# One half step of the attention behind every half group of the first two expert units

## Chip, cores and metric

The kernel runs on one core of a Trainium2 chip. The metric is the device time of one execution in microseconds, the median of the runs. The page of the profile names the engines as PE (TensorE), DVE (VectorE), ACT (ScalarE), POOL (GpSimd) and SP (SyncE, which issues most DMAs). "L500" is line 500 of the kernel before.

## What is computed

Three layers run one behind another on 1152 tokens (2 batches of 576).

```python
# attention, 8 heads of 64, on q, k, v [2, 8, 576, 64]
q_d, k_d, v_d = means over 4 neighbouring positions          # 144 positions
out_up = repeat(softmax(q_d @ k_d.T / 8) @ v_d, 4)           # the coarse part
out_local = softmax(mask(|i - j| < 4, q @ k.T / 8)) @ v      # the local part
x = (out_up + out_local) as [1152, 512]
# experts: P [1152, 8] from exp(x @ w_gate), 8 rounds of row and column normalization
out = sum over e of P[:, e] * (relu(x @ w1[e]) @ w2[e])      # w1[e] 512 x 1024, w2[e] 1024 x 512
# gated layer
result = ((out @ w_a) * (out @ w_b)) @ w_out                 # inner width 1536
```

## The kernel before

All large products keep float32 accuracy in three passes: both factors are split into a high and a low part (`xh`, `xl` for the tokens, `hi`, `lo` for the weights, `gh`, `gl` for the hidden layer) and hi·hi, lo·hi and hi·lo are summed in PSUM. An expert is cut into two units of 512 hidden columns; there are 16 units and then 6 units of the gated layer.

**The stage of the change** is the part in which attention and the first two expert units share the engines. Tokens come in three blocks of 384 (`NB`, `TB`). For a block and a unit there are four groups (`g_plain`, `f` = 0 to 3): 12 matmuls of 384 columns (4 contraction tiles by 3 passes, `g_part`) into one PSUM bank, then the relu on ScalarE (L500, writes `gh`) and the low part on VectorE (L501, writes `gl`). Then come three output tiles for each unit (`o_moe`, `o_mm`): 12 matmuls of 512 columns each, and one VectorE instruction adds the result to `acc` (L541, L543). Groups and tiles use two PSUM banks in turn.

**Attention** is a software pipeline in the generator `side()`. `order` lists 24 steps (a batch, a third of its positions, a pair of heads); eight of them bring new keys (third 0): indices 0, 2, 4, 6, 10, 12, 14 and 15. Iteration `s` has two half steps, each ended by a `yield`:

- first half: loads for step s+2 on SP (`load_q`, `load_k`, `load_v`); `a1(s)` transposes the queries on TensorE (L990), and where the step brings keys also six key tiles (L1004); `c3(s-3)` and `a2(s)` are copies out of PSUM on ScalarE (L1148; keys L1011, L1012; queries L1023); `b4(s-2)` is four VectorE instructions (L1111, L1112, L1115, L1119) and one on GpSimd (L1116); `d3` is one on ScalarE (L1185) and one on GpSimd (L1186); `b2(s-1)` is two maxima on VectorE (L1089, L1092); `a3(s)` sums keys (L1048, where there are new ones) and queries (L1037) over four positions on VectorE.
- second half, for s from 11 (`TURN`) on: `a4(s)` scales the summed keys on ScalarE (L1059); TensorE then runs `b1(s)` (a mask matmul, then local scores; needs the queries of `a2`), `d1(s-3)` (values), `b1c(s)` (coarse scores, tile `kd`; needs the sums of `a3` and `a4`) and `c1(s-2)` (transposes of the softmax, L1129, L1134); `d2a` and `b3` run on ScalarE (L1169, the exponentials L1099 and L1102), `d2` and `c2` on VectorE (L1175, L1140).

When a block of tokens is complete, `logits` follows in two halves: eight matmuls and a copy on ScalarE (L1203), then three transposes (L1208) and a copy. Attention's own PSUM tiles rotate through six banks (`psa`). Each engine takes its instructions in the order in which this Python program writes them down.

**What sets the order.** After every group and every output tile the loop calls `step()` (L1472). It adds `SIDE` = 1.5 to `turn` and, if two are due, runs two half steps one directly behind the other, with one piece of weight preparation (`run_first`: a cast on ScalarE, L138, and a subtraction on VectorE, L139) written between them; in the steady pattern that is none, two, two, two. A pair that starts inside the pipeline is the second half of one step and the first half of the next. `load_some`, called once for each half step, hands one weight DMA to SP. Up to the first block (23 half steps) attention runs without this loop, with two groups of block 0 filled in by `g_early`; at the start of block 1 two groups are opened (9 of 12 matmuls) ahead of the loop (`begun`). Before the third block the attention is closed and the gating of the experts takes the place of the half steps (`mid`).

Of the kernel before, what the change touches and what calls it, by code (L numbers as in the profile page):

```python
# [8 lines left out]
F32 = mybir.dt.float32  # L9
# [11 lines left out]
def attn_moe_glu_kernel(  # L21
# [16 lines left out]
    nc = tc.nc  # L38
# [6 lines left out]
    KT = DM // 128  # L45
# [34 lines left out]
    ident = const.tile([128, 128], F32, name="ident")  # L80
# [249 lines left out]
    for i, w in enumerate((w_a, w_b, w_out)):  # L330
        t = dram.tile(list(w.shape), F32, name=f"w32_{i}")
# [86 lines left out]
    units = []  # L418
    for e in range(E):
        for hf in range(2):  # L420
            u = Unit()
# [8 lines left out]
    for g in range(GU):  # L430
        u = Unit()
# [21 lines left out]
    def g_part(u, ps, b, f, kts):  # L453

        cols = slice(b * TB, (b + 1) * TB)
        for kt in kts:
            w = u.w[f // 2, kt // 2]
            o = (kt % 2) * 256 + (f % 2) * 128
            a_h, a_l = w.hi[:, o:o + 128], w.lo[:, o:o + 128]
            parts = (a_h, xh), (a_l, xh), (a_h, xl)  # L460
            for k, (l, r) in enumerate(parts):
                mm(ps, l, r[:, kt, cols], kt == 0 and k == 0, kt == KT - 1 and k == 2)
        M.pe += 0.52 * len(kts)

    def g_open(u, b, f):
        ps = bank("g")[:, :TB]
        g_part(u, ps, b, f, range(KT - 1))
        return ps

    def g_early(u, b, banks):  # L470
# [14 lines left out]
                if kt < KT - 1:  # L485
                    yield

    def g_plain(u, n, b, f, mid, ps=None, full=False):

        gh, gl = GP[0][n], GP[1][n]  # L490
        if ps is None:
            ps = g_open(u, b, f)
        if not full:
            g_part(u, ps, b, f, (KT - 1,))
        for j in range(2):
            u.w[f // 2, j].use()
        if closed:
            pump(0.0)
        mid()
        nc.scalar.activation(out=gh[:, f], in_=ps, func=AF.Relu)  # L500
        nc.vector.scalar_tensor_tensor(  # L501
            out=gl[:, f], in0=ps, scalar=0.0, in1=gh[:, f].bitcast(F32),
            op0=ALU.max, op1=ALU.subtract,
        )
        act(0.5)
        dve(0.56)

    def o_mm(u, gh, gl, t):
        ps = bank("o")
        k = 0  # L510
        for f in (0, 2, 3, 1) if u.no == 4 else (0, 1):
            sl = slice(t * 128, (t + 1) * 128)
            a_h, a_l = gh[f][:, sl], gl[f][:, sl]
            w = u.o[f]
            for l, r in ((a_h, w.hi), (a_h, w.lo), (a_l, w.hi)):
                mm(ps, l, r, k == 0, k == 3 * u.no - 1)
                k += 1
        M.pe += 0.683 * u.no
        for w in u.o:
            w.use()  # L520
        return ps

    def o_moe(u, gh, gl, t, tt, mid=None, first=False):
        if u.e > 0:
            while gens[0] is not None:
                side_step()
        ps = o_mm(u, gh, gl, t)
        if mid:
            if closed:
                pump(0.0)  # L530
            mid()
        if not first:
            pump()
        a = acc[tt]
        if u.e == 0:
            if u.hf == 0 and closed:
                nc.scalar.copy(out=a, in_=ps)
                act(0.65)
                return
            if u.hf == 0:  # L540
                nc.vector.tensor_copy(out=a, in_=ps)  # L541
            else:
                nc.vector.tensor_tensor(out=a, in0=ps, in1=a, op=ALU.add)  # L543
        else:
            if u.e == 1 and u.hf == 0:
                nc.scalar.mul(out=a, in_=a, mul=P[:, tt, 0:1])
                act(0.65)
            nc.vector.scalar_tensor_tensor(  # L548
                out=a, in0=ps, scalar=P[:, tt, u.e:u.e + 1], in1=a, op0=ALU.mult, op1=ALU.add
            )  # L550
        dve(0.76)
        if first:
            pump()
# [328 lines left out]
    at = attn_stack.enter_context(tc.tile_pool(name="at", bufs=3, side="right"))  # L882
# [101 lines left out]

    def a1(i, b, u, hp):

        pq = psa.tile([128, 512], F32, tag="at", name="at")
        qn = q_nat.pop((b, u, hp))
        for j in range(2):
            nc.tensor.transpose(  # L990
                pq[:, j * 96:(j + 1) * 96], qn[:, j].rearrange("p h d -> p (h d)"), ident[:96, :96]
            )
        pk = pk2 = None
        if not i:
            warm(1)
        if u == 0:
            kn = k_nat[b, hp]
            pk = pq[:, 192:480]
            if not i:
                pk = psa.tile([128, 512], F32, tag="at", name="at")[:, 0:288]  # L1000
            pk2 = psa.tile([128, 512], F32, tag="at", name="at")
            for j in range(6):
                o = (pk if j < 3 else pk2)[:, j % 3 * 96:j % 3 * 96 + 96]
                nc.tensor.transpose(o, kn[:, j].rearrange("p h d -> p (h d)"), ident[:96, :96])  # L1004
        pA[i] = pq, pk, pk2

    def a2(i, b, u, hp):
        pq, pk, pk2 = pA.pop(i)
# [252 lines left out]
    def side():  # L1261
        n = len(order)
        done_l = 0

        def do(st, j):
            if 0 <= j < n:
                st(j, *order[j])

        for s in range(n + 5):
            if s == 5:  # L1270
                wg32 = load_gate()
            if s == 9:
                gate_weights(wg32)
            if s + 2 < n:
                load_q(s + 2)
                if order[s + 2][1] == 0:
                    load_k(order[s + 2][0], order[s + 2][2])
            if s in FETCH_VD:
                load_vd(0, FETCH_VD.index(s))
            if s in LOAD_V:  # L1280
                load_v(LOAD_V[s])
            last = s >= 4 and (s - 3) % (2 * HP) == 0
            do(a1, s)
            if s <= TURN:
                do(b1, s - 1)
                do(b1c, s - 1)
            if last:
                do(d3, s - 4)
            do(c3, s - 3)
            do(a2, s)  # L1290
            do(b4, s - 2)
            if not last:
                do(d3, s - 4)
            do(b2, s - 1)
            do(a3, s)
            yield
            do(a4, s)
            if s >= TURN:
                do(b1, s)
            do(d1, s - 3)  # L1300
            if s >= TURN:
                do(b1c, s)
            do(d2a, s - 3)
            do(b3, s - 1)
            do(c1, s - 2)
            do(d2, s - 3)
            do(c2, s - 2)
            if s in SUM_VD:
                sum_vd(0, SUM_VD.index(s))
            if 0 <= s - 2 < n and order[s - 2][:2] == (1, 0):  # L1310
                sum_vd(1, order[s - 2][2])
            if 0 <= s - 1 < n and order[s - 1][:2] == (1, 0):
                load_vd(1, order[s - 1][2])
            yield
            while done_l <= ready[0]:
                yield from logits(done_l)
                done_l += 1
                yield

    TURN = 11  # L1320
    FRONT = 10
    V_PAIRS = (0, 2, 4, 6, 16, 18, 20, 22)
    PAIRS = V_PAIRS[2:]
# [30 lines left out]
    with tc.manual_schedule():  # L1354
# [58 lines left out]
        def run_first(n):  # L1413
            while n and wq:
                if len(units[1].o) == 4 and (wq[0].slot or not wq[0].ok()):
                    return
                n -= run(wq).slot
# [52 lines left out]
        share = [0, 0, 1, 1, 1, 1, 2, 2, 1, 2, 1]  # L1470

        def step():  # L1472
            nonlocal turn
            if not closed:
                turn += SIDE
                n = 0
                while n < 2 and (turn >= 2 or n):
                    turn -= 1
                    side_step()
                    n += 1  # L1480
                    if n == 1:
                        run_first(share.pop(0) if share else 1)
                if not n:
                    run_first(share.pop(0) if share else 1)
            else:
                pump()

        def mid():
            if closed:
# [4 lines left out]
        for b in range(NB):  # L1494
# [23 lines left out]
            for n in range(2):  # L1518
                while len(units[n].w) < 2:
                    run_first(1)  # L1520
                full = bool(begun)
                if n == 0 and not closed and not full:
                    begun = {f: g_open(units[n], b, f) for f in range(2)}
                for f in range(4):
                    while len(units[n].w) < 4 and f > 1:
                        run_first(1)
                    g_plain(units[n], n, b, f, mid, begun.get(f), full and f < 2)
                    step()
                begun = {}
            per = TB // 128  # L1530
            firsts = [[
                lambda n=n, t=t, b=b: o_moe(
                    units[n], *([G[n][:, f] for f in range(4)] for G in GP), t, b * per + t, mid)
                for t in range(per)
            ] for n in range(2)]
            for n in range(2 if b < NB - 1 else 1):
# [145 lines left out]
```

## Time and profile before

| | |
|---|---|
| median of 3 runs | 1052.09 us (1051.04 to 1054.85) |
| the profiled execution: its time | 1052.0 us |
| its span, first to last instruction | 1050.2 us |
| granted TensorE clock, mean | 1.000 |
| TensorE busy (matmuls) | 1040.3 us |
| VectorE, ScalarE, GpSimd busy | 657.7, 481.3, 527.2 us |

The span is what the profile shows; 1.8 us lie around it. A row of a timeline gives the start, the duration, the engine, the line, the tiles written and read, the shape and the count; what stands in brackets is the engine's idle time before it and what ended it. A matmul's duration is longer than the distance to the next one, because matmuls overlap: distances between starts tell what the stream costs.

### The profile page before, as it was taken

To read this page: it belongs to the slowest core of one execution; us is meant where nothing else is said; L and a number is where in the kernel's file an instruction comes from. 1 tells how busy PE (TensorE), PEld (TensorE's weight loads), DVE (VectorE), ACT (ScalarE), POOL (GpSimd) and SP (SyncE) were. 2 spreads that over 40 slices of the span, in tenths; PEclk is the share of its full clock that TensorE was granted. 3 is DMA by queue.
4 is the path that set the end of the run, shared out by engine and by line. 5 is a ranking of instruction groups with operands and counts; after the bars stand their busy time and mean duration, and the time that the engine had idled before them with its cause. 6 is when DMAs were issued, how large, how long until landed. Compare 5 with 4: busy or idle time off the path is not lost.

```text
span 1050.2 us, 18523 instructions
## 1 busy us (share of the span) xinstructions
PE 1040.3 (99%) x6940; PEld 938.0 (89%) x6940; DVE 657.7 (63%) x1333; ACT 481.3 (46%) x1168; POOL 527.2 (50%) x531
## 2 busy tenths in 40 slices
PE   8999999999999999999999999999999999999998
PEld 6887888989998998999899998999899899999997
DVE  7785638666566565656665565656544685767664
ACT  6764514664454444445444454545333744333320
POOL 5533236646474644647465554646444545655521
PEclk9999999999999999999999999999999999999999
DMA  9552001242423323242333323232210102221002
GB/s 191 147 150 73 16 1 41 71 129 67 128 83 112 102 89 105 66 127 84 109 91 103 105 66 106 85 117 83 71 61 21 41 21 61 61 61 41 31 11 90
DMA packets 80728, 84.53 MB, mean 80 GB/s; under 512 B 35328, under 2 KB 54784, under 8 KB 80640
## 3 DMA queue, kind: packets, MB, share of 16 engines
q1 hardware_dynamic: 79456, 83.07, 26.8%
q8 instruction: 54, 0.88, 0.3%
q10 hardware_dynamic: 1184, 0.30, 0.1%
q14 instruction: 34, 0.28, 0.1%
HBM read 71.54 MB, written 11.80 MB: 79 GB/s over the span
## 4 chain that ended last, share of the span: by engine, by line
PE 94%; DVE 3%; DMA 1%; ACT 1%; issue 1%; SPq 0%; POOL 0%; DVEq 0%; ACTq 0%
PE g L61 89%; PE at L61 3%; DMA kn<-in_k_dram 1%; PE at L1129 1%; PE at L1134 1%; DMA vw<-in_v_dram 0%; PE g L855 0%; DVE w L139 0%; DVE kd L1048 0%; DMA raw<-w 0%; ACT w L138 0%; DVE pdn L1119 0%; PE at L990 0%; ACT p L1099 0%; DVE rsum L1111 0%
## 5 line engine op out<-in xcount | busy, mean ns | idle before, releaser
L61 PE MATMUL g<-w,gh 128*128 128x512 f32 x1314 | 407.8, 391 | 0.0
L61 PE MATMUL g<-xh,w 128*128 128x256 f32 (+2 forms) x1472 | 315.9, 300 | 0.0
L692 POOL TENSOR_TENSOR gl<-G,gh 128x256 fp32r<-128x256 f32 (+1 forms) x216 | 178.1, 834 | 249.8 <-ACT gh L690 243.7
L61 PEld LDWEIGHTS g<-w,gh 128*128 128x128 f32 x1314 | 239.3, 188 | 44.0 <-DVE w L139 0.3
L61 PE MATMUL g<-w,gl 128*128 128x512 f32 x657 | 257.2, 392 | 0.0
L61 PEld LDWEIGHTS g<-xh,w 128*128 128x128 f32 x1472 | 242.6, 188 | 2.4
L61 PE MATMUL g<-xl,w 128*128 128x256 f32 (+2 forms) x736 | 219.7, 299 | 0.0
L696 DVE TENSOR_TENSOR G<-g,G 128x256 f32<-128x256 f32 (+1 forms) x400 | 168.3, 451 | 68.6 <-PE g L61 36.7
L61 PE MATMUL g<-Th,w 128*128 128x256 f32 (+1 forms) x960 | 207.4, 293 | 0.3 <-DVE G L696 0.2
L139 DVE TENSOR_TENSOR w<-raw,w 128x512 fp32r<-128x512 f32 x129 | 116.6, 914 | 79.8 <-ACT w L138 79.2
L61 PEld LDWEIGHTS g<-Th,w 128*128 128x128 f32 x960 | 159.6, 188 | 3.3 <-issue 0.9
L548 DVE SCALAR_TENSOR_TENSOR acc<-g,P,acc 128x512 f32<-128x512 f32 x126 | 94.2, 748 | 94.1 <-PE g L61 90.7
L61 PEld LDWEIGHTS g<-w,gl 128*128 128x128 f32 x657 | 123.3, 188 | 26.4
L61 PE MATMUL g<-Tl,w 128*128 128x256 f32 (+1 forms) x480 | 140.5, 293 | 0.0
L61 PEld LDWEIGHTS g<-xl,w 128*128 128x128 f32 x736 | 138.0, 188 | 2.6 <-issue 0.2
L690 ACT CAST gh<-G 128x256 fp32r<-128x256 f32 (+1 forms) x216 | 93.7, 434 | 100.7 <-DVE G L706 85.8
L138 ACT CAST w<-raw 128x512 fp32r<-128x512 f32 x181 | 109.7, 622 | 62.2 <-POOL raw L269 47.7
L688 ACT ACTIVATE G<-G 128x256 f32<-128x256 f32 (+1 forms) x168 | 74.2, 442 | 103.1 <-DVE G L696 103.1
L139 POOL TENSOR_TENSOR w<-raw,w 128x512 fp32r<-128x512 f32 x52 | 68.5, 1326 | 58.3 <-ACT w L138 58.3
L61 PEld LDWEIGHTS g<-Tl,w 128*128 128x128 f32 x480 | 90.2, 188 | 2.1
L381 POOL TENSOR_TENSOR dec<-dec 128x384 int32<-128x384 int32 x48 | 49.5, 1031 | 77.5 <-ACT dec L357 52.3
L139 POOL TENSOR_TENSOR w<-s,w 128x512 fp32r<-128x512 f32 x40 | 55.7, 1393 | 21.1 <-ACT w L138 21.0
(178 smaller groups left out, 992.4 us busy)
## 6 DMA issues: line engine op xcount, KB each, us to landing
raw<-in_moe_w_dram SPq DMA_DIRECT2D x128, 256.0 KB
w<-dec SPq DMA_DIRECT2D x48, 192.0 KB
dec<-in_moe_w_a_dram SPq DMA_DIRECT2D x16, 384.0 KB
dec<-in_moe_w_b_dram SPq DMA_DIRECT2D x16, 384.0 KB
dec<-in_moe_w_out_dram SPq DMA_DIRECT2D x16, 384.0 KB
raw<-w SPq DMA_DIRECT2D x48, 128.0 KB
raw<-w SPq DMA_DIRECT2D x12, 256.0 KB
out_dram<-acc SPq DMA_DIRECT2D x9, 256.0 KB
```

What stands on the lines that cost most here:

```text
L61: nc.tensor.matmul(out=o, lhsT=l, rhs=r, start=start, stop=stop, skip_group_check=not check)
L138: nc.scalar.copy(out=hi, in_=raw)
L139: lows.append(lambda: (low or nc.vector).tensor_tensor(out=lo, in0=raw, in1=hi.bitcast(F32), op=ALU.subtract))
L381: nc.gpsimd.tensor_tensor(out=t, in0=t, in1=raw[:, :, 0], op=ALU.add)
L548: nc.vector.scalar_tensor_tensor(out=a, in0=ps, scalar=P[:, tt, u.e:u.e + 1], in1=a, op0=ALU.mult, op1=ALU.add)
L688: nc.scalar.activation(out=src, in_=src, func=AF.Relu)
L690: nc.scalar.copy(out=h, in_=src)
L692: nc.gpsimd.tensor_tensor(out=l, in0=src, in1=h.bitcast(F32), op=ALU.subtract)
L696: nc.vector.tensor_tensor(out=o, in0=bank_, in1=b, op=ALU.add)
L1129: nc.tensor.transpose(pt2[0:72, kh * 128:kh * 128 + R], pd.rearrange("p (t k) -> p k t", k=2)[:, kh], ident[:R, :R],)
L1134: nc.tensor.transpose(pt[0:W, c * 128:(c + 1) * 128], p[:, c], ident)
```

## The change

The groups and output tiles of the first two units get a place in their middle (behind 6 of 12 matmuls) at which a half step may run, next to the one at their end. `turn` now grows by 0.75 at each of the two places and at most one half step runs at one place, so three of four places have one. `run_first` stays at the end of the group, now behind the half step. The groups of `begun` have no middle place, so the two blocks of the loop have 26 places each. The keys of the steps 12, 14 and 15 (`SOON`) are transposed by the new `a0` at the end of the second half of the step before, into PSUM tiles that are taken there; `a1` then transposes only their queries.

```diff
--- before.py
+++ after.py
@@ -462,9 +462,12 @@
                 mm(ps, l, r[:, kt, cols], kt == 0 and k == 0, kt == KT - 1 and k == 2)
         M.pe += 0.52 * len(kts)
 
-    def g_open(u, b, f):
+    def g_open(u, b, f, piece=None):
         ps = bank("g")[:, :TB]
-        g_part(u, ps, b, f, range(KT - 1))
+        g_part(u, ps, b, f, range(2))
+        if piece:
+            piece()
+        g_part(u, ps, b, f, range(2, KT - 1))
         return ps
 
     def g_early(u, b, banks):
@@ -485,11 +488,11 @@
                 if kt < KT - 1:
                     yield
 
-    def g_plain(u, n, b, f, mid, ps=None, full=False):
+    def g_plain(u, n, b, f, mid, ps=None, full=False, piece=None):
 
         gh, gl = GP[0][n], GP[1][n]
         if ps is None:
-            ps = g_open(u, b, f)
+            ps = g_open(u, b, f, piece)
         if not full:
             g_part(u, ps, b, f, (KT - 1,))
         for j in range(2):
@@ -505,7 +508,7 @@
         act(0.5)
         dve(0.56)
 
-    def o_mm(u, gh, gl, t):
+    def o_mm(u, gh, gl, t, piece=None):
         ps = bank("o")
         k = 0
         for f in (0, 2, 3, 1) if u.no == 4 else (0, 1):
@@ -515,16 +518,18 @@
             for l, r in ((a_h, w.hi), (a_h, w.lo), (a_l, w.hi)):
                 mm(ps, l, r, k == 0, k == 3 * u.no - 1)
                 k += 1
+            if piece and k == 6:
+                piece()
         M.pe += 0.683 * u.no
         for w in u.o:
             w.use()
         return ps
 
-    def o_moe(u, gh, gl, t, tt, mid=None, first=False):
+    def o_moe(u, gh, gl, t, tt, mid=None, first=False, piece=None):
         if u.e > 0:
             while gens[0] is not None:
                 side_step()
-        ps = o_mm(u, gh, gl, t)
+        ps = o_mm(u, gh, gl, t, piece)
         if mid:
             if closed:
                 pump(0.0)
@@ -984,25 +989,38 @@
 
     def a1(i, b, u, hp):
 
-        pq = psa.tile([128, 512], F32, tag="at", name="at")
+        if i in SOON:
+            pq, pk, pk2 = pA[i]
+        else:
+            pq = psa.tile([128, 512], F32, tag="at", name="at")
         qn = q_nat.pop((b, u, hp))
         for j in range(2):
             nc.tensor.transpose(
                 pq[:, j * 96:(j + 1) * 96], qn[:, j].rearrange("p h d -> p (h d)"), ident[:96, :96]
             )
+        if i in SOON:
+            return
         pk = pk2 = None
         if not i:
             warm(1)
         if u == 0:
-            kn = k_nat[b, hp]
             pk = pq[:, 192:480]
             if not i:
                 pk = psa.tile([128, 512], F32, tag="at", name="at")[:, 0:288]
             pk2 = psa.tile([128, 512], F32, tag="at", name="at")
-            for j in range(6):
-                o = (pk if j < 3 else pk2)[:, j % 3 * 96:j % 3 * 96 + 96]
-                nc.tensor.transpose(o, kn[:, j].rearrange("p h d -> p (h d)"), ident[:96, :96])
+            keys_in(k_nat[b, hp], pk, pk2)
         pA[i] = pq, pk, pk2
+
+    def keys_in(kn, pk, pk2):
+        for j in range(6):
+            o = (pk if j < 3 else pk2)[:, j % 3 * 96:j % 3 * 96 + 96]
+            nc.tensor.transpose(o, kn[:, j].rearrange("p h d -> p (h d)"), ident[:96, :96])
+
+    def a0(i, b, u, hp):
+        if i in SOON:
+            pq, pk2 = (psa.tile([128, 512], F32, tag="at", name="at") for _ in range(2))
+            pA[i] = pq, pq[:, 192:480], pk2
+            keys_in(k_nat[b, hp], pA[i][1], pk2)
 
     def a2(i, b, u, hp):
         pq, pk, pk2 = pA.pop(i)
@@ -1305,6 +1323,7 @@
             do(c1, s - 2)
             do(d2, s - 3)
             do(c2, s - 2)
+            do(a0, s + 1)
             if s in SUM_VD:
                 sum_vd(0, SUM_VD.index(s))
             if 0 <= s - 2 < n and order[s - 2][:2] == (1, 0):
@@ -1318,6 +1337,7 @@
                 yield
 
     TURN = 11
+    SOON = (12, 14, 15)
     FRONT = 10
     V_PAIRS = (0, 2, 4, 6, 16, 18, 20, 22)
     PAIRS = V_PAIRS[2:]
@@ -1470,20 +1490,19 @@
         share = [0, 0, 1, 1, 1, 1, 2, 2, 1, 2, 1]
 
         def step():
+            if not closed:
+                piece()
+                run_first(share.pop(0) if share else 1)
+            else:
+                pump()
+
+        def piece():
             nonlocal turn
             if not closed:
-                turn += SIDE
-                n = 0
-                while n < 2 and (turn >= 2 or n):
+                turn += SIDE / 2
+                if turn >= 1:
                     turn -= 1
                     side_step()
-                    n += 1
-                    if n == 1:
-                        run_first(share.pop(0) if share else 1)
-                if not n:
-                    run_first(share.pop(0) if share else 1)
-            else:
-                pump()
 
         def mid():
             if closed:
@@ -1524,13 +1543,13 @@
                 for f in range(4):
                     while len(units[n].w) < 4 and f > 1:
                         run_first(1)
-                    g_plain(units[n], n, b, f, mid, begun.get(f), full and f < 2)
+                    g_plain(units[n], n, b, f, mid, begun.get(f), full and f < 2, piece)
                     step()
                 begun = {}
             per = TB // 128
             firsts = [[
                 lambda n=n, t=t, b=b: o_moe(
-                    units[n], *([G[n][:, f] for f in range(4)] for G in GP), t, b * per + t, mid)
+                    units[n], *([G[n][:, f] for f in range(4)] for G in GP), t, b * per + t, mid, False, piece)
                 for t in range(per)
             ] for n in range(2)]
             for n in range(2 if b < NB - 1 else 1):
```

## Rows read from the trace of the kernel before

**Rows 1.** The page, part 1: busy time, share of the span, instructions

```profile
PE 1040.3 (99%) x6940; PEld 938.0 (89%) x6940; DVE 657.7 (63%) x1333; ACT 481.3 (46%) x1168; POOL 527.2 (50%) x531
```

**Rows 2.** By stage: us; busy PE, PEld, DVE, ACT, POOL; clock; DMA share; GB/s

```profile
38.70:96.90 58.20, 56.89 (x595) 48.63 (x594) 41.81 (x111) 34.14 (x112) 21.10 (x30) 1.00 0.53 138
96.90:146.70 49.80, 49.12 (x435) 42.37 (x433) 22.96 (x66) 18.44 (x60) 13.17 (x20) 1.00 0.04 10
```

**Rows 3.** Timeline of TensorE: first matmuls and coarse scores of steps 12, 15, 17, 20, 21

```profile
49.35 0.28 PE L61 MATMUL at<-mask,identb 128*64 128x210 bf16 x2
...
50.89 0.45 PE L61 MATMUL at<-kd,qT 128*64 128x144 f32 x4 [0.30 <-DVE qT L1037]
...
66.70 0.28 PE L61 MATMUL at<-mask,identb 128*64 128x210 bf16 x2
...
68.36 0.45 PE L61 MATMUL at<-kd,qT 128*64 128x144 f32 x4 [0.43 <-ACT od L1169]
...
80.27 0.28 PE L61 MATMUL at<-mask,identb 128*64 128x210 bf16 x2
...
81.64 0.46 PE L61 MATMUL at<-kd,qT 128*64 128x144 f32 x4
...
101.84 0.28 PE L61 MATMUL at<-mask,identb 128*64 128x210 bf16 x2
...
104.11 0.46 PE L61 MATMUL at<-kd,qT 128*64 128x144 f32 x4 [0.67 <-DVE qT L1037]
...
109.54 0.28 PE L61 MATMUL at<-mask,identb 128*64 128x210 bf16 x2
...
110.60 0.41 PE L61 MATMUL at<-kd,qT 128*64 128x144 f32 x4
```

**Rows 4.** Timeline of TensorE: where groups, tiles and query transposes begin

```profile
47.06 0.59 PE L61 MATMUL g<-xh,w 128*128 128x384 f32 x2
...
77.34 0.71 PE L61 MATMUL g<-w,gh 128*128 128x512 f32 x2
...
105.08 0.33 PE L990 MATMUL at<-ident,qn 96*128 96x96 f32 x2
105.19 0.60 PE L61 MATMUL g<-xh,w 128*128 128x384 f32 x2
```

**Rows 5.** Timeline of ScalarE and VectorE from a group's end to step 20's sums

```profile
100.79 0.49 ACT L500 ACTIVATE gh<-g 128x384 fp32r<-128x384 f32 x1 [3.19 <-PE g L61]
...
101.32 0.56 DVE L501 SCALAR_TENSOR_TENSOR gl<-g,gh 128x384 fp32r<-128x384 f32 x1 [5.50 <-ACT gh L500]
...
101.91 0.37 DVE L1111 TENSOR_REDUCE rsum<-p 128x3 f32<-128x213 f32 x1
...
103.51 0.54 DVE L1037 TENSOR_REDUCE qT<-qT 128x96 f32<-128x384 f32 x1
```

**Rows 6.** Timeline of VectorE in step 15, which brings keys: first and last

```profile
65.40 0.37 DVE L1111 TENSOR_REDUCE rsum<-p 128x3 f32<-128x213 f32 x1
...
67.67 0.54 DVE L1037 TENSOR_REDUCE qT<-qT 128x96 f32<-128x384 f32 x1
```

**Rows 7.** Timeline around the second logits: groups start, copy on ScalarE

```profile
96.93 0.51 PE L61 MATMUL g<-xh,w 128*128 128x384 f32 x2
97.13 0.47 ACT L1203 COPY lt<-at 16x384 f32<-16x384 f32 x1 [1.13 <-PE at L61]
```

**Rows 8.** Timeline around the keys of step 14: last exponential, key transposes

```profile
58.36 0.40 ACT L1102 ACTIVATE pd<-at,nd 112x144 f32<-112x144 f32 x1
58.47 0.66 PE L1004 MATMUL at<-ident,kn 96*128 96x96 f32 x6
```

**Rows 9.** Timeline of SP: DMAs of the keys of step 12

```profile
36.79 1.00 SPq L926 DMA_DIRECT2D kn<-in_k_dram  x2
```

**Rows 10.** Timeline behind the loop: GpSimd's last sum of tokens, VectorE's first use

```profile
139.61 1.31 POOL L613 TENSOR_TENSOR b<-xh,xl 128x512 f32<-128x512 f32 x1
...
150.07 0.68 DVE L621 TENSOR_TENSOR t<-b,t 128x512 f32<-128x512 f32 x1
```

## Prediction, made before the changed kernel was built

> **What bounds the kernel now.** I read the page's busy times first, then a table of the stages, then the timeline of TensorE in the stage of the change, and last the timelines of the engines on which TensorE waits there. TensorE's matmuls cover 99% of the span, VectorE 63%, ScalarE 46% [rows 1]; the changed stage, 38.7 to 146.7 us, looks no different: TensorE is covered for 56.89 of 58.20 and 49.12 of 49.80 us, at a granted clock of 1.00, the 2.4 GHz level [rows 2]. A microsecond that TensorE loses or saves there moves the end by a microsecond, since everything behind is TensorE's stream too. What the coverage hides, the starts show. From the first matmul of a second half step to its coarse scores TensorE needs 1.06 us where nothing is late (109.54 to 110.60). It took 1.54 in step 12, 1.66 in step 15 (step 14 is its twin), 1.37 in step 17 and 2.27 in step 20 [rows 3]. Less 1.06 each, five stalls make 0.48 + 0.60 + 0.60 + 0.31 + 1.21 = 3.20 us. They end when VectorE has summed the queries or ScalarE has scaled the keys. That is all that the change can win: 0.3% of the time.
>
> **The change, part by part.** It moves half steps and adds no arithmetic.
>
> *Old stalls.* Each would go if its first half lay far enough ahead of its second half. Count: with 0.75 a place, one place in four is empty, so two half steps lie one half group apart, or two where the empty place falls between. First and second half of a step are then one half group apart in the steps 12, 14, 15, 17, 18, 20, 22 and 23 and two in 13, 16, 19 and 21. Before, a whole group (sometimes two) lay between them, except in step 20, which had three matmuls. Only step 20 gets more.
>
> *TensorE's path between the two halves.* Two groups' worth of starts give 47.06 to 49.35 = 2.29 us for 12 matmuls [rows 4], and 105.19 to 109.54 = 4.35 for 24 [rows 3, 4], so six matmuls are (4.35 − 2.29) / 2 = 1.03, and a run of six with its two borders 2.29 − 1.03 = 1.26. The query transposes before it take 0.11 (105.08 to 105.19) plus something for the group ahead of them; I take 0.2. With 1.06 up to the coarse scores TensorE arrives 0.2 + 1.26 + 1.06 = 2.52 us after the group's end. A tile of 12 takes 77.34 to 80.27 = 2.93 [rows 3, 4]; half of it makes the path 0.2 + 1.5 + 1.06 = 2.76.
>
> *The chain that it meets.* Where the first half stands at a group's end, its work is queued behind that group's relu and low part on ScalarE and VectorE. From L500 to L501 are 0.53, L501 holds VectorE's queue for some 0.47 (0.59 to the next listed start, where a small logits copy lies between), and from the start of L1111 to the end of the query sums are 2.14 [rows 5], and with keys 2.81 [rows 6]. TensorE resumes 0.06 after the sums without keys and 0.15 with them [rows 3, 5, 6]. With 0.1 ahead of L500 the chain is 0.1 + 0.53 + 0.47 + 2.14 + 0.06 = 3.3 us, with keys 4.06. ScalarE's copies and the scaling of keys run beside it. `run_first`, which stood between the halves of a pair on both engines, now stands behind the first half; I have left it out of this chain.
>
> *New stalls*, chain less path. Step 12 (keys, group's end): 4.06 − 2.52 = 1.5. Step 15 (the same, but half a tile between): 4.06 − 2.76 = 1.3. Steps 20 and 23 (no keys): 3.3 − 2.52 = 0.8 each. Step 14 stands in a group's middle, with no relu ahead: 2.81 + 0.15 − 2.52 = 0.4. Step 18 stands behind a tile, which puts one instruction less ahead: between 0 and 0.8, I take 0.2. Steps 17 and 22 (middle, no keys) and the four with two half groups: 2.14 + 0.06 is below the path; I take 0.1 for 17, where weight splits share VectorE. The logits of block 1 now have three matmuls between their halves: the copy ends at 97.60, 0.67 behind the last logits matmul's successor at 96.93 [rows 7]; three matmuls are 0.5, so 0.2. Sum 1.5 + 1.3 + 1.6 + 0.4 + 0.2 + 0.1 + 0.2 = 5.3 us against 3.2 before: **+2.1**. Behind each waiting matmul stand the rest of the half step and the next half group, although its operands are there; VectorE's lists end before the next group's relu needs it.
>
> *Borders.* A pair broke into a group once, single half steps do it each. In block 0 there were 10 places with TensorE work for 20 half steps, now 19 for 19: +9. In block 1 the first halves of 20 to 23 stand alone now: +4. A run of 12 with borders takes 2.29 where 2 × 1.03 = 2.06 would be without: 0.23 is the most that one more break can cost. The least is near 0.05, because most of that belongs to the second half step's border, which exists already. I take 0.1, nearer the low end for that reason: **+1.3** (0.7 to 3.0).
>
> *Keys sooner.* The transposes are moved, not removed: they no longer stretch TensorE's path inside the step, and they no longer hold ScalarE's copies. Two PSUM tiles are taken when the exponentials of the step before may still read one. Before, the keys of step 14 began at 58.47 while the last exponential ran from 58.36 to 58.76 [rows 8], with no wait to be seen. Bounds 0 to 0.4 each, since such an exponential ends 0.4 after it starts; I take 0.1, three times: **+0.3**. The keys of step 12 are asked of SP at 36.79 [rows 9]; their transposes ended just ahead of the group at 47.06 [rows 4] and are now due some 4.5 us sooner, still about 5 us after the issue.
>
> *Queues and what follows.* SP issues the same DMAs in the same order and is held by free buffers, not by the place of a half step; GpSimd's products and low parts stay hidden behind at least a half group. The loop holds 39 half steps instead of 42; the missing three are empty ones and run at the start of the third block. The last sums of tokens on GpSimd start later by about two tiles (2 × 2.93 = 6 us), since the last step's result is two places later; before they ended at 140.92 and VectorE first used one at 150.07 [rows 10], so 9 us cover them, and a lost cover would cost what exceeds that. Zero.
>
> Sum: 2.1 + 1.3 + 0.3 = +3.7. The profiled execution took 1052.0 us, so 1055.7; the median of the runs lies 0.1 above it: **1055.8 us**.
>
> One rule speaks the other way. The Trainium skill, "Perfetto Trace Analysis", section "Optimization Strategy", says that where the most contended engine changes between regimes, interleaving the regimes can improve performance. By it the stalls would vanish and only the borders be paid, rival A's 1050.2 us. The trace so far is against it at this grain: 3.3 us of chain meet 2.52 us of path [rows 3 to 5].
>
> **The rivals.**
>
> *A. Finer mixing fills the stalls (faster).* If VectorE had its share of a first half done within the path of 2.5 us, the old 3.2 would go and the borders be paid: −3.2 + 1.3 = −1.9, 1050.2 us. It decides at 2.5 us between a group's end and the query sums. For it: VectorE is idle for a quarter to a half of these stages (41.81 of 58.20 and 22.96 of 49.80 us busy) [rows 2]. Against it: the chain of 3.3 was measured in one piece in step 20 [rows 5], whose stall was 1.21 with three matmuls between; three more are 0.5. 17%.
>
> *B. The gains and losses nearly meet.* If the new stalls are half of what I sum (2.7) and the borders at their low end (0.7), the result is 2.7 − 3.2 + 0.7 = +0.2: about 1052.3, between 1051.3 and 1053.3. 10%.
>
> *C. Something is late that the sum does not hold (slower by more).* PSUM tiles for the keys at 0.4 each (+0.9 over my term), borders at 0.2 (+1.3) or a weight half that ScalarE waits for in order, with the attention copies behind it; DMA has a share of 0.53 in block 0 [rows 2]. Together +5.5 to +7: 1057.5 to 1059. Against it: no wait of ScalarE on a weight DMA lies in this stage now. 13%.
>
> **How the numbers follow.** My forecast, 1053.3 to 1057.4, has 60%. The range takes it whole, B, and the better half of A and of C: 1050.2 to 1058.2 us. A measurement of this kernel can tell about 0.5% (5.3 us) from no change. Faster than 1046.8 would need more than all stalls: 2%. Slower than 1057.4 is C and the forecast's edge: 15%. Within: 83%.
>
> **What would show it.** Right: runs of six matmuls on TensorE between half steps; coarse scores waiting for VectorE or ScalarE in steps 12, 15, 20 and 23, 0.8 to 1.5 us each; block 1 ending 3 to 4.5 us later than 146.7; the rest of the kernel as long as before. Wrong: coarse scores 1.06 us behind the mask matmul in those steps; a chain from L500 to the query sums much shorter than 3.2; key transposes that wait for an exponential; a difference behind the third block's start.

## The result and the profile after

The changed kernel takes **1060.47 us** (median of 6 runs, 1059.25 to 1062.54) against 1052.09: a ratio of 1.008, 95% interval 1.0069 to 1.0091. It is slower by 8.4 us, more than twice the forecast's 3.7 and outside the range. The profiled execution took 1060.08 us, with a span of 1058.3. Some executions of most kernels here, the kernel before among them, have a mean granted clock of 0.993 to 0.997 and take 2 to 5 us longer than the others; the medians hold them as they came.

The page of the changed kernel, part 1, against [rows 1]:

```profile
PE 1043.8 (99%) x6940; PEld 940.0 (89%) x6940; DVE 658.6 (62%) x1333; ACT 481.1 (45%) x1168; POOL 526.8 (50%) x531
```

Same instruction counts, same covered share. The table by stage says where the time lies (us; busy time of PE, PEld, DVE, ACT, POOL; granted clock; DMA share; GB/s):

```profile
38.69:101.65 62.96, 58.52 (x587) 48.53 (x586) 42.56 (x110) 34.13 (x110) 21.53 (x30) 0.97 0.50 127
101.65:154.50 52.85, 51.10 (x443) 43.89 (x440) 23.98 (x70) 18.81 (x63) 13.02 (x20) 1.00 0.04 9
154.50:1058.30 903.80, 899.18 (x5419) 819.50 (x5419) 562.49 (x1042) 401.75 (x902) 467.73 (x436) 1.00 0.25 77
```

Beside [rows 2] the two stages of the change grew from 58.20 to 62.96 and from 49.80 to 52.85 us. By their first matmuls (38.74 before, 38.69 after, to the third block's first group at 146.70 and 154.50) it is 107.96 against 115.81: **+7.85**. Behind it 903.80 us follow, 903.50 before. So the loss is in the stage named, and the larger part of it in block 0, where the granted clock is 0.97.

What the forecast spoke of is there. Timeline of TensorE, first in step 12, then in step 23 (the columns as in [rows 3]):

```profile
49.03 0.33 PE L998 MATMUL at<-ident,qn 96*128 96x96 f32 x2
49.14 0.60 PE L61 MATMUL g<-xh,w 128*128 128x384 f32 x2
...
50.37 0.28 PE L61 MATMUL at<-mask,identb 128*64 128x210 bf16 x2
...
53.17 0.45 PE L61 MATMUL at<-kd,qT 128*64 128x144 f32 x4 [0.71 <-ACT od L1187]
...
54.06 0.59 PE L61 MATMUL g<-xh,w 128*128 128x384 f32 x2
...
55.19 0.33 PE L998 MATMUL at<-ident,qn 96*128 96x96 f32 x2
...
127.61 0.28 PE L61 MATMUL at<-mask,identb 128*64 128x210 bf16 x2
...
129.66 0.46 PE L61 MATMUL at<-kd,qT 128*64 128x144 f32 x4 [0.55 <-DVE qT L1055]
```

From the mask matmul to the coarse scores, less the 1.06 of [rows 3], step 12 loses 53.17 − 50.37 − 1.06 = 1.74 (forecast 1.5) and step 23 loses 0.99 (0.8). Read in the same way, step 20 loses 0.99, 14 0.38, 17 0.29 and 18 0.26: 4.65 in all, 3.20 before, so +1.45. Step 15 takes 0.27 too long, but no wait is listed there; that belongs to the lower clock below. (The bracket of step 12 names L1187, which the program places behind the coarse scores. The last that these need are VectorE's sums, and they end at 53.03.) A half group with its borders takes 49.14 to 50.37 = 1.23, the other half 54.06 to 55.19 = 1.13.

What it did not speak of stands at unit 0's first output tile, which now holds the second half of step 15 in its middle; the first half of step 15 stands ahead of the tile. Timeline of all engines:

```profile
67.97 0.70 PE L61 MATMUL g<-w,gh 128*128 128x512 f32 x2
68.05 0.49 ACT L503 ACTIVATE gh<-g 128x384 fp32r<-128x384 f32 x1 [1.52 <-PE g L61]
...
69.38 0.68 ACT L1041 ACTIVATE qT<-at 64x192 f32<-64x192 f32 x2
...
70.34 1.13 ACT L138 CAST w<-raw 128x512 fp32r<-128x512 f32 x2
...
71.01 0.49 PE L61 MATMUL g<-w,gh 128*128 128x512 f32 x1 [2.10 <-ACT w L138]
...
71.77 1.28 DVE L139 TENSOR_TENSOR w<-raw,w 128x512 fp32r<-128x512 f32 x2
...
72.51 0.50 PE L61 MATMUL g<-w,gh 128*128 128x512 f32 x1 [1.01 <-DVE w L139]
...
73.17 0.28 PE L61 MATMUL at<-mask,identb 128*64 128x210 bf16 x2
...
74.50 0.70 PE L61 MATMUL at<-kd,qT 128*64 128x144 f32 x4
...
78.09 0.33 PE L998 MATMUL at<-ident,qn 96*128 96x96 f32 x2
```

and the same place in the kernel before:

```profile
69.02 1.16 ACT L138 CAST w<-raw 128x512 fp32r<-128x512 f32 x2
...
69.44 0.71 PE L61 MATMUL g<-w,gh 128*128 128x512 f32 x2
...
71.01 0.63 PE L61 MATMUL g<-w,gh 128*128 128x512 f32 x2
```

In the changed kernel six matmuls take 67.97 to 73.17 = 5.20 us. The tile sums the blocks in the order 0, 2, 3, 1: after three matmuls it needs block 2 of the output weights, whose cast (L138) now starts at 70.34, behind the group's relu (68.05) and six ScalarE instructions of the half step (copies, and the scaling of the queries at 69.38). ScalarE worked without a gap from 68.05 to the cast, so it waited for no transfer. In the kernel before, this cast started at 69.02, between the two half steps of a pair and ahead of the second one's copies, and the same six matmuls took 69.44 to 71.01 = 1.57. So the tile lost **3.63** us. The two waits, with one matmul between them, have a second price. The table by window, in the columns of the stage table:

```profile
70.00:74.00 4.00, 1.99 (x29) 1.32 (x31) 3.06 (x7) 1.73 (x5) 1.10 (x2) 0.99 0.55 134
74.00:78.00 4.00, 4.00 (x29) 3.19 (x26) 0.71 (x2) 1.58 (x6) 0.00 (x0) 0.59 0.27 70
78.00:82.00 4.00, 4.00 (x44) 3.14 (x43) 3.64 (x9) 1.52 (x4) 2.17 (x3) 1.00 0.00 0
```

For some 4 us the granted clock averages 0.59, most of it at the 1.2 GHz level. In the 4 us before that, TensorE was busy for 1.99 us.

The last item is the third block's start. Timeline of TensorE:

```profile
153.54 0.35 PE L1226 MATMUL at<-ident,lt 16*128 16x16 f32 x3
...
154.50 0.62 PE L61 MATMUL g<-xh,w 128*128 128x384 f32 x2 [0.61 <-DVE lg L1227]
```

The second logits of block 2 now stand last in the stage, and the group behind them waits until VectorE has read them: 0.96 from their transposes to the group; before, the matmuls behind them started after 0.28 (143.53 to 143.81): +0.7.

**The sum.** Stalls +1.45, tile +3.63, lower clock +1.51 (0.27 in step 15 and 1.24 that the first experiment measures), third block's start +0.68, and 0.33 that the keys of step 14 wait for a PSUM tile, until an exponential (L1120) has read it: 7.6 of 7.85.

### The profile page after: what moved, and what is told of

It reads as the page before. It is cut to its first block, busy times and chain, and to the rows that moved or that the text cites. A ratio compares the mean times of both kernels' runs of the same rounds, so it can differ in the third digit from the quotient of the medians.

```text
span 1058.3 us, 18511 instructions
## 1 busy us (share of the span) xinstructions
PE 1043.8 (99%) x6940; PEld 940.0 (89%) x6940; DVE 658.6 (62%) x1333; ACT 481.1 (45%) x1168; POOL 526.8 (50%) x531
## 4 chain that ended last, share of the span: by engine, by line
PE 94%; DVE 2%; DMA 2%; ACT 1%; issue 0%; SPq 0%; POOL 0%; ACTq 0%; DVEq 0%
PE g L61 89%; PE at L61 3%; DMA kn<-in_k_dram 1%; DMA vw<-in_v_dram 1%; PE at L1147 1%; PE at L1152 1%; DMA rv<-in_v_dram 0%; PE g L860 0%; DVE gl L504 0%; PE at L1017 0%; DMA raw<-w 0%; DVE qT L1055 0%; DVE nm L1107 0%; ACT gh L503 0%; ACT p L1117 0%
## 5 line engine op out<-in xcount | busy, mean ns | idle before, releaser
L138 ACT CAST w<-raw 128x512 fp32r<-128x512 f32 x181 | 109.6, 621 | 62.9 <-POOL raw L269 48.4
```

What stands on the lines that cost most here:

```text
L138: nc.scalar.copy(out=hi, in_=raw)
```

## The experiments

Theory: the split of weights behind the half step starves the output tile; the clock's fall follows from that. Rivals: the DMA of the weights is late (rival C as written), or the early keys are what costs. The kernel before, run beside them on the same chip, took 1052.57, 1052.71 and 1052.68 us in the three batches.

**1. The changed kernel, but the tile takes its blocks as they are prepared** (of the divided tiles only):

```diff
-        for f in (0, 2, 3, 1) if u.no == 4 else (0, 1):
+        for f in (0, 1, 2, 3) if piece else (0, 2, 3, 1) if u.no == 4 else (0, 1):
```

> The changed kernel, but the tiles of the first two units sum their four weight blocks in the order 0, 1, 2, 3 instead of 0, 2, 3, 1. Theory (the weight splits now stand behind a half step on ScalarE and VectorE, and the first tile waits for block 2): its first six matmuls need only blocks 0 and 1, which were split a group earlier. The waits of 2.1 and 1.0 us go, the clock does not fall behind them (about 1.1 us), and step 15's own stall of about 1 us comes back: 1056.0 to 1057.5 us. Rival (the weight DMAs land late): the tile waits as long in its second half, about 1060 us.

Measured: 1056.69 us (9 runs, 1055.59 to 1057.12), ratio 1.0033 (1.0023 to 1.0044), span 1053.8. Timeline of TensorE in this kernel:

```profile
67.33 0.71 PE L61 MATMUL g<-w,gh 128*128 128x512 f32 x2
...
68.90 0.28 PE L61 MATMUL at<-mask,identb 128*64 128x210 bf16 x2
...
71.37 0.45 PE L61 MATMUL at<-kd,qT 128*64 128x144 f32 x4 [0.72 <-ACT od L1187]
...
73.72 0.33 PE L998 MATMUL at<-ident,qn 96*128 96x96 f32 x2
```

The half tile is back at 68.90 − 67.33 = 1.57, and step 15's own stall, which the tile's wait had covered, shows: 71.37 − 68.90 − 1.06 = 1.41, forecast 1.3. From the coarse scores to the next query transposes it is now 2.35 us; in the changed kernel, at the lower clock, the same work took 74.50 to 78.09 = 3.59. That 1.24, with the 0.27 in step 15, is the price of the clock. Together 3.63 + 1.51 − 1.41 = 3.7, and the two stages differ by 115.81 − 112.03 = 3.78. One edit that touches no DMA takes away the whole surprise, and ScalarE waited for no transfer ahead of the cast, so a late transfer is refuted as its cause. What is left, 1056.69, is within 0.9 us of the forecast, in part by luck: stalls and third block's start cost more than forecast, borders less. The stage is 112.03 us long, +4.07: stalls 6.07 − 3.20 = 2.87, keys 0.33, third block's start 0.7, which leaves a remainder of 0.2 for the 13 new borders and the logits of block 1.

**2. The changed kernel with the split ahead of the half step:**

```diff
-                piece()
                 run_first(share.pop(0) if share else 1)
+                piece()
```

> The changed kernel, but at a group's end the weight splits are written ahead of the half step, not behind it. Theory: the first tile's wait and the fall of the clock go (about -4.7 us together), but the splits stand in VectorE's chain of the steps 12 (one) and 15 (two), whose coarse scores wait 0.6 and about 2 us longer than without: about 1058 us, between the changed kernel and the one with the other order of blocks. Rival (distance between the halves does not matter): the whole 4.7 us are won, 1055.8 us or less.

Measured: 1061.32 us (4 runs, 1059.92 to 1062.87), ratio 1.0079 (1.0058 to 1.01). Timeline of TensorE in steps 12 and 14 of this kernel:

```profile
50.22 0.28 PE L61 MATMUL at<-mask,identb 128*64 128x210 bf16 x2
...
53.66 0.45 PE L61 MATMUL at<-kd,qT 128*64 128x144 f32 x4 [0.85 <-ACT od L1187]
...
63.62 0.28 PE L61 MATMUL at<-mask,identb 128*64 128x210 bf16 x2
...
66.09 0.46 PE L61 MATMUL at<-kd,qT 128*64 128x144 f32 x4 [0.97 <-ACT kd L1077]
```

The tile's two waits shrink from 2.1 and 1.0 to 0.2 each, as expected, but the splits now stand ahead of the half step's own copies and sums: step 12 loses 3.44 − 1.06 = 2.38, step 14 1.4, step 15 1.7, and step 13, which lost nothing, 0.6. Size missed by 3 us. Against experiment 1 step 12 loses the 0.6 more that was expected, step 15 only 0.3 more instead of 2; the 1.0 more in step 14, the 0.6 in step 13 and 0.7 that early keys wait for a PSUM tile were not priced at all.

**3. The kernel before with only the splits moved**, behind both half steps of a pair; no half step moves:

```diff
-                    if n == 1:
-                        run_first(share.pop(0) if share else 1)
-                if not n:
-                    run_first(share.pop(0) if share else 1)
+                run_first(share.pop(0) if share else 1)
```

> The kernel before, but the weight splits are written behind both half steps of a pair instead of between them. Theory: the first tile waits for block 2 here too, 2 to 3 us, since the splits of the last group stand behind a whole first half; the coarse scores of steps 12, 14, 15 and 17 wait about 0.5 us less each: net +0.5 to +1.5, 1052.6 to 1053.6 us. Rival (the place of the splits is not what matters): only the second part, about 1050.3 us.

Measured: 1060.9 us (4 runs, 1059.72 to 1062.59), ratio 1.0076 (1.0055 to 1.0097). Waits of TensorE from 38 to 160 us (what it waited for: us in total, times, longest):

```profile
PE g L61 <- ACT w L138: 3.1, 3, 1.2
PE g L61 <- DVE w L139: 2.1, 4, 0.8
PE g L61 <- DVE we L139: 0.7, 1, 0.7
...
PE g L61 <- ACT we L138: 0.6, 1, 0.6
```

Mechanism right, size far too small. Groups and tiles wait 6.5 us for weights, in nine places, where the kernel before has no such wait listed. The stalls of the coarse scores shrink from 3.20 to 1.44, about as expected, and the granted clock falls here too (0.50 from 56 to 58 us, behind waits of 0.89 and 0.80), which adds to the loss. In the changed kernel only one tile is hit; that its half steps are spread and leave shorter lists ahead of a split is my explanation, which no run tests. Put behind a whole pair, `run_first` alone costs as much as the whole change did, and its place was costed at nothing.

**4. and 5. The early keys undone**, in the changed kernel and in that of experiment 1:

```diff
-    SOON = (12, 14, 15)
+    SOON = ()
```

> The changed kernel with the keys of steps 12, 14 and 15 transposed in their own step, as before the change. Theory (the transposes are moved and cover as much where they stood): the wait of 0.3 us for a PSUM tile goes, the rest evens out: 1059.5 to 1060.7 us. Rival (the sooner keys shorten ScalarE's copies ahead of the scores): 1061.5 us or more.

> The changed kernel with the weight blocks of the first units' tiles in the order 0, 1, 2, 3 and with the keys of steps 12, 14 and 15 transposed in their own step. It tells what the sooner keys are worth where no clock fall blurs it. Theory (they are moved work; the 0.3 us wait of step 14's keys for a PSUM tile goes, the rest evens out): 1056.0 to 1057.2 us, as with the sooner keys (1056.7). Rival (the sooner keys spare the scores a wait): 1057.7 us or more.

Measured: 1062.64 us (4 runs, 1059.16 to 1063.71), ratio 1.0084 (1.0054 to 1.0113), and 1058.13 us (4 runs, 1055.51 to 1059.38), ratio 1.0045 (1.0028 to 1.0063). Both intervals overlap those of their partners (1.0069 to 1.0091 and 1.0023 to 1.0044), and the medians settle nothing: in both profiled executions the granted clock fell ahead of the stage, where neither kernel differs from its partner. Window of experiment 5's kernel (the clock is 1.00 there in experiment 1):

```profile
24.00:28.00 4.00, 4.00 (x47) 3.21 (x45) 1.75 (x5) 2.00 (x9) 1.82 (x2) 0.50 0.98 181
```

The stage itself can be compared, from step 11's mask matmul to the last logits. TensorE in experiment 1's kernel, then in experiment 5's:

```profile
39.85 0.28 PE L61 MATMUL at<-mask,identb 128*64 128x210 bf16 x2
...
149.15 0.35 PE L1226 MATMUL at<-ident,lt 16*128 16x16 f32 x3
```

```profile
44.70 0.28 PE L61 MATMUL at<-mask,identb 128*64 128x210 bf16 x2
...
152.83 0.35 PE L1226 MATMUL at<-ident,lt 16*128 16x16 f32 x3
```

That is 109.30 against 108.13 us: the early keys cost 1.2 us, which neither theory nor rival had. Without them the steps 12 and 15 lose 1.26 and 0.91 instead of 1.74 and 1.41, step 14 0.63 instead of 0.37, and the wait of 0.33 is gone. Transposed in their own step, the keys fill time in which TensorE would otherwise wait. In experiment 4 a lower clock in the tile blurs the same comparison. The early keys are not the cause of the 3.8 us that experiment 1 takes away.

**6. The changed kernel with the splits one piece sooner**, the order 0, 2, 3, 1 kept:

```diff
-        share = [0, 0, 1, 1, 1, 1, 2, 2, 1, 2, 1]
+        share = [0, 1, 1, 1, 1, 2, 2, 1, 2, 1]
```

> The changed kernel with the order of weight blocks as it was (0, 2, 3, 1), but every weight split done one group sooner. Theory (the first tile's wait is a matter of when the splits are queued): the wait is gone in another way, the clock does not fall, step 15 waits 1.4 us by itself: 1056 to 1057.5 us, as with the other order. Rival (the DMAs that bring the weights set the time): a split waits for its DMA, and the time stays above 1058.5 us.

Measured: 1058.6 us (4 runs, 1056.96 to 1059.29), ratio 1.0051 (1.0036 to 1.0065), granted clock 1.0 throughout. Timelines of ScalarE (first line) and TensorE in this kernel:

```profile
61.70 0.62 ACT L138 CAST w<-raw 128x512 fp32r<-128x512 f32 x1 [0.94 <-DMA raw<-in_moe_w_dram]
...
63.05 0.28 PE L61 MATMUL at<-mask,identb 128*64 128x210 bf16 x2
...
65.92 0.45 PE L61 MATMUL at<-kd,qT 128*64 128x144 f32 x4 [0.84 <-DVE qT L1055]
...
69.63 0.71 PE L61 MATMUL g<-w,gh 128*128 128x512 f32 x2
...
71.19 0.28 PE L61 MATMUL at<-mask,identb 128*64 128x210 bf16 x2
```

The half tile takes 71.19 − 69.63 = 1.56 with the order untouched, so a sooner cast feeds it as well as another order of the sum does. But the sooner cast meets its DMA: ScalarE waits 0.94 for the weights with step 14's copies behind it, VectorE's subtraction and sums follow late, and step 14 loses 2.87 − 1.06 = 1.81. The time misses the theory's range and lies at the rival's bound of 1058.5. Rival C's mechanism exists, one piece of weights sooner than the change puts it.

**7. A whole group between the two halves of a step.** The kernel of experiment 1 with the splits of experiment 6 and, in place of `turn`, a rule: a place behind a first half stays empty (two places in three have a half step).

```diff
-                turn += SIDE / 2
-                if turn >= 1:
-                    turn -= 1
+                if apart[0]:
+                    apart[0] = 0
+                else:
                     side_step()
```

(`apart[0]` is set at the end of a first half and cleared at the end of a second.)

> The changed kernel with blocks in the order 0, 1, 2, 3 and every split one group sooner, and another rule for the places: behind a first half step of the steps 12 to 23 one place is left empty, all others are used, so that a step's halves always lie two half groups apart. Theory (half a group is too short for VectorE's chain, a whole one nearly long enough): of the 6.1 us of waiting coarse scores some 1.5 are left, in the steps with keys, and the second logits of the last block come a place sooner, which spares the third block's first group 0.7: 1050.5 to 1053 us. Rival (VectorE as a whole is what binds, and the waits only move): 1055 us or more.

Measured: 1052.61 us (12 runs, 1051.86 to 1055.15), ratio 1.0004 (0.9995 to 1.0013). Waits of TensorE from 38 to 150 us:

```profile
PE at L1017 <- DVE x L1193: 1.2, 1, 1.2
PE at L61 <- ACT kd L1077: 0.8, 1, 0.8
PE at L61 <- DVE qT L1055: 0.5, 1, 0.5
```

As expected, the stalls of the steps 15, 17, 20 and 23 are gone; 12 and 14 keep one. New is 1.2 at L1017: the early keys of step 15 wait for their PSUM tile, three times the 0.4 that I had set as the bound.

**8. The kernel before, with only its irregular places mended**: `turn` half a unit lower at block 1's start, so that step 20 gets a whole group, and the splits spread otherwise.

```diff
-        share = [0, 0, 1, 1, 1, 1, 2, 2, 1, 2, 1]
+        share = [1, 0, 1, 0, 2, 0, 2, 2, 2, 0, 2]
...
+            if b == 1:
+                turn -= 0.5
```

> The kernel before with two changes of place: at the start of block 1 the pair behind the second opened group is put off by one group, so that step 20's halves no longer have three matmuls between them, and the weight splits stand where no pair does, as far as the weights are there. Theory: the wait of 1.2 us of step 20 goes, and 0.3 to 0.6 each of the steps 14 and 17: 1049.6 to 1050.9 us. Rival (another wait takes their place): 1051.5 us or more.

Measured: 1052.1 us (12 runs, 1051.16 to 1056.91), ratio 1.0 (0.9985 to 1.0014). Timeline of TensorE in the steps 15 and 20 of this kernel:

```profile
66.39 0.28 PE L61 MATMUL at<-mask,identb 128*64 128x210 bf16 x2
...
68.66 0.45 PE L61 MATMUL at<-kd,qT 128*64 128x144 f32 x4 [0.95 <-DVE qT L1037]
...
104.84 0.28 PE L61 MATMUL at<-mask,identb 128*64 128x210 bf16 x2
...
105.91 0.41 PE L61 MATMUL at<-kd,qT 128*64 128x144 f32 x4
```

Step 20's 1.21 is gone (105.91 − 104.84 = 1.07), but step 15 pays 2.27 − 1.06 = 1.21 where it paid 0.60, and one tile (82.62 to 86.32) takes some 0.75 longer than the 2.93 of [rows 3, 4], with a listed wait of 0.2 for weights: the rival's case. Here a split that left one place fell on another.

**9. and 10. Experiment 7 with the splits spread once more**, without the early keys (9) and with them (10):

```diff
-        share = [0, 1, 1, 1, 1, 2, 2, 1, 2, 1]
+        share = [0, 1, 1, 1, 1, 0, 2, 2, 1, 2, 1]
...
-    SOON = (12, 14, 15)
+    SOON = ()
```

> The variant with halves always two half groups apart, with the first two splits of unit 0's output weights one group later again and the keys of steps 12, 14 and 15 in their own step. Theory (the sooner keys cost a wait for a PSUM tile and win nothing where the halves lie a whole group apart): the 1.4 us wait of step 15's keys goes, and the 0.7 and 0.9 us left in steps 12 and 14 shrink by about half: 1050.0 to 1051.5 us. Rival (what one wait gives up another takes): 1052 us or more.

> The same with the sooner keys of the change kept. Theory: as the variant before it, but step 15's keys still wait for a PSUM tile if ScalarE or VectorE is late there: 1051 to 1052.6 us, about 1 us above the one with the keys in their own step. Rival (the wait came from the two splits alone): no difference between the two.

Measured: the ninth takes **1049.56 us** (6 runs, 1048.82 to 1050.45), ratio 0.9969 (0.9957 to 0.9981), 3.1 us less than the kernel before and the fastest of all; the tenth 1051.28 (12 runs, 1049.63 to 1054.39), ratio 0.9988 (0.9977 to 0.9999). Stage of the change in the ninth, in the columns of [rows 2]:

```profile
38.94:144.10 105.16, 105.07 (x1028) 90.25 (x1027) 65.76 (x177) 53.30 (x171) 34.96 (x50) 1.00 0.32 82
```

The stage takes 105.16 us against 107.96 before, and no wait of TensorE is listed in it; 0.2 each are left of the stalls of steps 12 and 14. That is 2.8 of the 3.2 us that the forecast called all there is to win. In the tenth the profile lists 1.0 us of waits for the query sums. Its interval touches the ninth's, but read as in experiment 5 its stage is again 1.2 us longer (41.46 to 144.24 against 40.70 to 142.30): the early keys cost here too.

## Why the prediction was wrong

**The step that failed** is the one in "The chain that it meets": "`run_first` ... now stands behind the first half; I have left it out of this chain." Left out of the chain it could be; what was missing is the other side. The split moved behind a half step on two in-order queues, and the forecast did not ask who waits for its product. That was unit 0's first output tile, which reads block 2 after three matmuls: 3.63 us, and 1.51 of lower clock behind it, less the 1.41 of step 15's stall that lay under the wait. Experiment 1 gave these 3.7 us back with one line, experiment 6 gave the half tile back by another. Rival C named "a weight half that ScalarE waits for in order", but as a late DMA; here ScalarE was late for TensorE.

**Path and chain** were right. Where nothing else disturbed them the stalls came near what was worked out: step 12 1.74 (1.5), 14 0.37 (0.4), 15 1.41 in experiment 1 (1.3), 20 and 23 0.99 (0.8 each), 17 and 18 0.29 and 0.28 (0.1 and 0.2). In experiment 1 they add up to 2.87 more than before, where +1.9 was forecast (the 2.1 less 0.2 for the logits of block 1). In step 12 the path was 49.03 to 50.37 and 1.06 more, 2.40 (2.52), and the chain 49.03 to 53.17, 4.14 (4.06): each was off by some 0.1, in the direction that lengthens the stall.

**Borders** were mis-sized: +1.3 forecast for 13 of them, 0.2 left in experiment 1's account for them and block 1's logits. A half group costs 1.23 and 1.13, in sum 0.07 more than the whole group's 2.29 of [rows 4], and from the softmax transposes to what follows them it is 0.08 less (53.81 to 54.06; 104.75 to 105.08 before). By that account the lower bound of 0.05 was itself too high.

**Keys sooner**: 0.33 of waiting at one place where 0.1 at each of three was taken, +0.3 in both; that the sum agrees is luck. Experiment 5 puts the whole price at 1.2, most of it inside the stalls above: a path that is made shorter only waits longer for the same chain. The bound of 0.4 for one place did not hold in experiment 7 (1.2): the tile's last reader there is not the exponential that I had looked at but VectorE's L1193.

**What follows**, costed at zero, cost 0.7: the second logits moved to the last place of the stage, and with them the wait for their copy. The sign "a difference behind the third block's start" missed it by one instruction: 903.80 against 903.50 from that start on.

**Rival A's** mechanism is real, at another grain. The Trainium skill, "Perfetto Trace Analysis", section "Optimization Strategy", says that interleaving regimes may improve performance. At half a group between the halves the runs speak against it (+4 us in experiment 1, 2.9 of them stalls), at a whole group for it (−3.1 us in experiment 9, which also has the other order of blocks and no early keys). What decides here is whether the work between the halves is longer than the chain: 2.5 us of path in the one against 3.5 to 4.3 of chain (the path plus the stalls of the steps 20 and 12), no listed wait in the other.

## What to carry to other kernels

A step that is moved past another on an in-order queue has two bills: what it now waits behind, and who waits for what it makes; list the reader of every product of a moved instruction, with the first instruction that reads it. Two halves that exchange work with other engines need between them at least the longest chain through those queues, and in this kernel a fixed distance held that better than a rate that leaves some places short. Work that is taken out of such a gap makes the wait longer, as the early keys did. Move work and preparation one at a time: in experiment 3 moving the preparation alone cost as much as the whole change.

## What the runs showed of the hardware

Two waits of 2.1 and 1.0 us, with one matmul between them, were followed by a granted clock of 0.59 over the next 4 us, between the levels of 1.2 and 2.4 GHz; the price was 1.24 us on 2.35 us of work, and 0.27 just ahead of it. That a stall of such size has a second price I had nowhere in the sum. In experiment 1, whose longest listed wait there is 0.72, the clock stayed at 1.00. The length of the listed waits alone does not tell when it falls: in experiment 3 waits of 0.89 and 0.80 were followed by 0.50 (56 to 58 us), but waits of 1.19, 0.23 and 0.72 later on by 1.00 (78 to 84 us), and in experiment 7 a single one of 1.18 by 1.00. What does tell stays open here. One more change between the groups' matmuls and the attention's, 13 times in the stage, left at most a remainder of 0.2 us in all; it was not measured by itself.
